# Rows loaded three blocks ahead, and the first two parts' work in another order, in a convolution and expert-MLP kernel

## The chip, the cores and the metric

The kernel runs on one core of a Trainium2 chip. The metric is the device time of one execution in microseconds (us). The engines of the core are TensorE (PE, with its weight loads shown as PEld), VectorE (DVE), ScalarE (ACT), GpSimd (POOL) and SyncE (SP). Each works through its own instructions in program order and waits on semaphores for the others. SP issues the loads (one queue, in order), POOL issues the indirect transfers that scatter rows.

## The reference

The input x has 8 sequences of 3584 tokens with 192 channels, 28672 tokens in all, in float32. First comes a causal convolution over 7 tokens whose taps are shared by the 24 channels of a head; then each token goes through one of 8 expert MLPs. A local gate decides whether the token takes its own best expert or that of the token before it, so the choice is a chain along the sequence.

```python
w = softmax(weight)                               # 8 heads x 7 taps
y[b, s, h*24:(h+1)*24] = sum_k w[h, k] * x_pad[b, s + k, h*24:(h+1)*24]

logits = y @ w_gate                               # 8 experts
local_gate = sigmoid(y @ w_local)
for b in range(B):
    prev_e = -1
    for s in range(S):
        fresh_e = argmax(logits[b, s])
        e = fresh_e if s == 0 or local_gate[b, s] < 0.5 else prev_e
        prev_e = e
        p = softmax(logits[b, s])
        out[b, s] = p[e] * (relu(y[b, s] @ w1[e]) @ w2[e])   # 192 -> 1024 -> 192
```

## The kernel before

The tokens are cut into 16 *parts* of 1792 tokens, 14 to a partition. Each part passes three steps, and the MLP follows in *blocks*.

**Convolution** (`conv`, L162). Where it is VectorE's, a head is one multiplication (`first`, on ScalarE at L177 or, for part 0, on VectorE at L175) and six multiply-adds on VectorE (L201). For parts 0 and 1, four of the eight heads (`ON_PE`: heads 5, 6, 7, 0) go to TensorE as products with diagonal matrices (L184), and ScalarE copies each result out (L187). The result is `y_sb`, whose last 64 columns repeat channels 128 to 191.

**Routing** (`route`, L262). `yr` takes channels 128 to 191 (L265), and L266 makes the repeat in `y_sb`, both on GpSimd. TensorE transposes the part (L280), ScalarE, or for every second tile of parts 0 and 1 VectorE, copies the transposes to `yT` (L282, L284), TensorE multiplies them with the gate weights (L291), ScalarE copies to `lsb` (L294, L295), TensorE transposes back (L299), VectorE takes `lt` (L303) and works through argmax, the chain along the sequence and the position of every token among those of its expert (to `posi`, L417). Then 14 *puts* are listed in `to_put`; each is one indirect transfer on GpSimd (`put`, L444) of 128 rows to their places in `slots` in DRAM, where rows lie by expert. Last come `base` (L421) and `table` (L455, some 20 small VectorE instructions), which ends in `tabi` (L512), the list of blocks that are sure to be full by then: first row and expert of each.

**Blocks.** There are 144: 35 single ones of 128 rows, 87 double ones of 256 rows, and 22 single ones at the end. Blocks 0 to 6 need part 0's rows alone, 7 to 20 part 1's too, 21 to 34 part 2's, 35 to 37 part 3's, 38 to 44 part 4's. Each block has its expert's weights `wb` (1536 KB, L565, four buffers) and rows `xg` (L572, six buffers), both loaded on SP's queue after SP has read the entry of `tabi`. `turn` transposes the rows on TensorE (L592) and VectorE copies them to `xT` (L595); `hidden` makes the hidden layer (L609, L613, Relu on ScalarE at L616); `output` multiplies back (L623), ScalarE scales with the gate (L629), and GpSimd scatters the rows to `out` (L632). Block i's instructions on TensorE are `hidden(i)`, `turn(i + 1)`, `output(i)`.

**The order.** Everything is issued in an order written out in the program, and each engine keeps to it. `conv` and `route` are generators: each yield gives the time that the instructions before it are reckoned to take on VectorE, or "hop" or "pe", where the route waits for TensorE and convolution work is put in. `step(time, scatters)` (L673) issues work of the current route and convolution up to that time, and so many puts; a single block has two steps of 2.1 with one put each, a double one two of 4.2 with one and two puts. `start_conv` (L643) also issues the load of the next part's x (L119, two buffers).

In the head (L695 to L713) part 0's route is issued with pieces of part 1's convolution at its hops; its puts follow at once, ahead of `base` and `table`; the rest of part 1's convolution comes next, then part 2's convolution is started (with it the load of x for part 3), and part 1's whole route is issued with eight pieces of part 2's convolution and its table. Its puts are left to the steps of the blocks. Then three weights and after them two blocks' rows are loaded (L728 to L731), and the blocks start.

In the loop, `ensure(i)` (L718) loads the weights of block i + 3 and then the rows of block i + 2. Where a block's part isn't routed, or some of its puts aren't issued yet, `ensure` issues steps of 4.2 until they are (L724).

Of the kernel before, what the change touches and what calls it, by code (L numbers as in the profile page):

```python
# [17 lines left out]
P = 128  # L18
B, S, D = 8, 3584, 192
# [33 lines left out]
Y0 = 2  # L53
# [29 lines left out]
def kernel(  # L83
# [8 lines left out]
    nc = tc.nc  # L92
# [31 lines left out]
    c = cst.tile([P, H, KC], F32, name="c")  # L124
# [19 lines left out]
    ON_PE = HEADS[:4]  # L144
# [117 lines left out]
    def route(g, alone):  # L262
        y_sb = got.pop(g)
        yr = yt.tile([P, NT, DR], F32, name="yr", bufs=2)
        nc.gpsimd.tensor_copy(yr, y_sb[:, :, Y0 + P:Y0 + D])  # L265
        nc.gpsimd.tensor_copy(y_sb[:, :, Y0 + D:], y_sb[:, :, Y0 + P:Y0 + D])  # L266

# [3 lines left out]
        for u in range(3):  # L271
            for jj in range(0, 4, 2):
                tps = (hps_p.tile([P, 2, BT], F32, name="hps") if alone and u else
                       bg_p.tile([P, 2, 2 * P], F32, name="bg"))
                for j in range(2):
                    for q in range(GQ):
                        t = min(2 * (4 * q + jj + j), NT - 2)
                        src = (yr[:, t:t + 2, :].rearrange("p t d -> p (t d)") if u == 2
                               else y_sb[:, t + u, Y0:Y0 + P])
                        nc.tensor.transpose(tps[:, j, q * P:(q + 1) * P], src, identity=ident)  # L280
                if alone and jj:
                    nc.vector.tensor_copy(yT[:, u, jj:jj + 2, :], tps)  # L282
                else:
                    nc.scalar.copy(yT[:, u, jj:jj + 2, :], tps)  # L284
            if not alone:
                yield "hop"
# [6 lines left out]
        m = 32 * (NP - 4)  # L293
        nc.scalar.copy(lsb[:m, :], lps[:m, :])  # L294
        nc.scalar.copy(lsb[m:, :P], lps[m:, :P])  # L295
        yield "hop"
        ltp = bg_p.tile([P, GQ * P], F32, name="bg")
        for q in range(GQ):
# [119 lines left out]
        for t in range(NT):  # L418
            to_put.append((g, y_sb[:, t, :], posi[:, t:t + 1]))
        yield 0.2  # L420
        nc.vector.tensor_tensor(base, base, nps[:, E:2 * E], op=Alu.add)  # L421
        yield 0.2
        was = g - 1 if g else None
# [8 lines left out]
    to_put = []  # L432
# [4 lines left out]
    def put():  # L437


        if not to_put:  # L440
            return
        g, rows, to = to_put.pop(0)
        nc.gpsimd.nop()
        ins = nc.gpsimd.indirect_dma_start(  # L444
            out=slots[:, :], in_=rows, in_offset=None,
            out_offset=bass.IndirectOffsetOnAxis(ap=to, axis=0)).ins
# [115 lines left out]
    def load_w(i):  # L562
        e = entry(i, 1, E - 1)
        wb = wp.tile([P, WA + WB], F32, name="wb")
        nc.sync.dma_start(out=wb, in_=w12[bass.ds(e, 1)].rearrange("o p x -> (o p) x"))  # L565
        return wb

    def load_rows(i):
        n, group = blocks[i][1], blocks[i][3]
        r = entry(i, 0, DUMMY + 1 - n)  # L570
        xg = xp.tile([P, KT, DG], F32, name="xg")
        get = nc.sync.dma_start(  # L572
            out=xg[:, :n, :].rearrange("p k d -> p (k d)"),
            in_=slots.rearrange("(r p) d -> r (p d)", p=UT)[bass.ds(r, n)]
            .rearrange("o (p x) -> (o p) x", x=n * DG))
# [22 lines left out]
    def hidden(n, wb, xT):  # L598
        hT = hp.tile([P, FK, BT], F32, name="hT")
        hps = [hps_p.tile([P, 2, BT], F32, name="hps") for q in range(FK // 2)]  # L600
        w = slice(0, n * P)


        for half in range(2):
            for j in range(2):
                for row in range(2):
                    rows = slice(row * DR, (row + 1) * DR)
                    f0 = F + (half * 2 + j) * P
                    nc.tensor.matmul(hps[half * 2 + row][:, j, w], lhsT=wb[rows, f0:f0 + P],  # L609
                                     rhs=xT[rows, 1, w], start=(j == 0), stop=False,  # L610
                                     skip_group_check=True)
# [31 lines left out]
    def start_conv(on_pe=()):  # L643
        g = st["conv"] + 1

        free = not any(p[0] <= g - 3 for p in to_put)
        if st["cgen"] is None and g < NPART and g <= st["route"] + LEAD and free:
            st["conv"] = g
            st["cgen"], st["pgen"] = conv(g, x_in.pop(g), on_pe)
            next(st["cgen"])  # L650
            if g + 1 < NPART:
                x_in[g + 1] = load_x(g + 1)

    def conv_op():
        c = next(st["cgen"], None) if st["cgen"] else None
        if c is None:
            st["cgen"] = None
        return c

    def start_route(alone=False):  # L660
        done = st["conv"] - (st["cgen"] is not None)
        if st["rgen"] is None and st["route"] < done:
            st["route"] += 1
            st["rgen"] = route(st["route"], alone)

    def route_op():
        c = next(st["rgen"], None)
        if c is None:
            st["rgen"] = None
            st["routed"] = st["route"]  # L670
        return c

    def step(time, scatters):  # L673

        start_route()
        start_conv()
        go = st["rgen"] is not None
        while time > 0:
            c = route_op() if go else conv_op()
            if c is None:  # L680
                if not go:
                    break
                go = False
            elif c == "hop":
                go = False
            elif c == "pe":
                c = conv_op()
                time -= c or 0
            else:
                time -= c  # L690
        for _ in range(scatters):
            put()


    start_route(True)  # L695
    start_conv(ON_PE)
    for g in range(2):
        while st["rgen"]:
            c_ = route_op()
            if c_ in ("hop", "pe"):  # L700
                conv_op()
            if c_ == "pe":
                for _ in range(3):
                    next(st["pgen"], None)
            while to_put and g == 0:
                put()
        for _ in st["pgen"]:
            pass
        if g == 0:
            while st["cgen"]:  # L710
# [74 lines left out]
```

## Time and profile before

| | us |
|---|---|
| time, median of 3 runs (lowest to highest) | 1500.04 (1499.82 to 1504.15) |
| the profiled execution's own time | 1495.5 |
| its span in the profile | 1493.8 |
| TensorE busy | 1443.5 (97%) |
| VectorE busy | 659.2 (44%) |
| ScalarE busy | 509.0 (34%) |
| GpSimd busy | 505.5 (34%) |

The profile records one execution. In its rows a time is counted from the span's start; a bracket at the end of a timeline row gives how long the engine sat idle before the instruction and what ended the wait. L numbers are lines of the kernel before. "issue" stands for waits that the profile doesn't explain. An average over the span hides that the stages differ: the head, where TensorE is mostly idle; the single blocks to about 330 us, with the highest traffic on the DMA queues; the double blocks, where TensorE is busy throughout; and the last single blocks.

### The profile page before, as it was taken

The page shows a single profiled execution, that of the slowest core. Times are in us where ns is not written, and L with a number is a line of the kernel's source. Part 1 is how long each engine was busy: PE and PEld are TensorE (multiplying, and loading weights), DVE is VectorE, ACT ScalarE, POOL GpSimd, SP SyncE. Part 2 cuts the span into 40 slices and gives each one's busy share as a digit, 9 for nine tenths or more (in the row PEclk, how much of TensorE's full clock was granted, in tenths as well). Part 3 has the DMA queues.
Part 4 walks back from the last instruction along what each step waited for, and adds up shares of the span by engine and source line. Part 5 has one row for each costly group of instructions (what it writes and reads, how often), then busy time and mean ns, then how long its engine had stood idle before and what let it go on. Part 6 is the DMA issues. An engine that isn't in the chain of part 4 may idle for free.

```text
span 1493.8 us, 25899 instructions
## 1 busy us (share of the span) xinstructions
PE 1443.5 (97%) x9792; PEld 1292.7 (87%) x9792; DVE 659.2 (44%) x1759; ACT 509.0 (34%) x1093; POOL 505.5 (34%) x526
## 2 busy tenths in 40 slices
PE   7588999999999999999999999999999999999998
PEld 4377898989889898898988888898898898899997
DVE  6778666666666666666666662400000000000000
ACT  3124434434343333433434333222222222223332
POOL 1433444434344343443444434343211211211111
PEclk9889999999999999999999999999999999999999
DMA  4577999987575665665656555665554554556883
GB/s 163 212 249 278 359 303 327 332 324 265 186 255 213 225 249 193 249 242 196 249 198 248 206 191 204 203 228 189 197 186 164 196 188 164 194 185 241 292 306 133
DMA packets 66415, 343.03 MB, mean 230 GB/s; under 512 B 12656, under 2 KB 23655, under 8 KB 45810
## 3 DMA queue, kind: packets, MB, share of 16 engines
q1 hardware_dynamic: 44064, 288.66, 55.5%
q0 software_dynamic: 22224, 52.70, 9.0%
q8 instruction: 78, 1.28, 0.3%
q14 instruction: 47, 0.39, 0.1%
q10 hardware_dynamic: 2, 0.00, 0.0%
HBM read 288.51 MB, written 53.49 MB: 229 GB/s over the span
## 4 chain that ended last, share of the span: by engine, by line
PE 54%; issue 30%; POOL 7%; DMA 5%; DVE 3%; POOLq 0%; SPq 0%; ACT 0%; DVEq 0%; ACTq 0%
PE yps L623 23%; PE hps L613 15%; PE hps L609 8%; POOL out_dram L632 5%; DMA xg<-slots 4%; POOL slots L444 2%; PE xps L592 2%; PE bg L280 2%; DVE y_sb L201 2%; PE bg L291 2%; PE hps L184 1%; DMA x_sb<-in_x_dram 1%; POOLq L632 0%; PE bg L299 0%; PE bg L390 0%
## 5 line engine op out<-in xcount | busy, mean ns | idle before, releaser
L623 PE MATMUL yps<-wb,hT 128*128 128x192 f32 x3696 | 626.7, 327 | 0.0
L623 PEld LDWEIGHTS yps<-wb,hT 128*128 128x128 f32 x3696 | 597.2, 190 | 1.9 <-issue 1.6
L632 POOL DMA_INDIRECT out_dram<-o_sb,xg x231 | 243.9, 1056 | 861.2 <-ACT o_sb L629 782.6
L613 PE MATMUL hps<-xT,wb 128*128 128x256 f32 (+1 forms) x2304 | 442.3, 345 | 0.0
L201 DVE SCALAR_TENSOR_TENSOR y_sb<-x_sb,c,y_sb 128x336 f32<-128x336 f32 x720 | 415.7, 587 | 25.5 <-ACT y_sb L177 8.3
L613 PEld LDWEIGHTS hps<-xT,wb 128*128 128x128 f32 x2304 | 365.0, 191 | 67.3 <-issue 29.1
L616 ACT ACTIVATE hT<-hps 128x512 f32<-128x512 f32 (+1 forms) x576 | 294.9, 512 | 348.3 <-PE hps L613 341.0
L595 DVE COPY xT<-xps 128x512 f32<-128x512 f32 (+1 forms) x144 | 84.3, 586 | 740.6 <-PE xps L592 740.6
L629 ACT ACTIVATE o_sb<-yps,xg 128x192 f32<-128x192 f32 x231 | 87.6, 418 | 554.0 <-PE yps L623 549.0
L444 POOL DMA_INDIRECT slots<-y_sb,posi x224 | 220.8, 986 | 100.8 <-issue 66.5
L609 PE MATMUL hps<-xT,wb 64*128 64x256 f32 (+1 forms) x2304 | 240.9, 349 | 6.5 <-DVE xT L595 6.5
L609 PEld LDWEIGHTS hps<-xT,wb 64*128 64x128 f32 x2304 | 183.4, 188 | 49.3 <-issue 17.3
L592 PE MATMUL xps<-ident,xg 128*128 128x128 f32 x462 | 74.8, 274 | 8.8 <-DMA xg<-slots 8.6
L592 PEld LDWEIGHTS xps<-ident,xg 128*128 128x128 f32 x462 | 57.3, 142 | 19.5 <-DMA xg<-slots 6.4
L177 ACT ACTIVATE y_sb<-x_sb,c 128x336 f32<-128x336 f32 x116 | 65.9, 580 | 0.4
L284 ACT COPY yT<-bg 128x512 f32<-128x512 f32 x86 | 46.2, 590 | 12.5 <-PE bg L280 12.5
L280 PE MATMUL bg<-ident,y_sb 128*128 128x128 f32 x240 | 33.5, 287 | 8.2 <-DVE y_sb L201 7.7
L184 PE MATMUL hps<-x_sb,wb 128*128 128x336 f32 x112 | 35.1, 473 | 3.8 <-DMA x_sb<-in_x_dram 3.8
L280 PEld LDWEIGHTS bg<-ident,y_sb 128*128 128x128 f32 x240 | 29.3, 149 | 10.2 <-issue 6.7
L184 PEld LDWEIGHTS hps<-x_sb,wb 128*128 128x128 f32 x112 | 22.3, 203 | 14.5 <-issue 5.5
L291 PE MATMUL bg<-yT,wg 128*32 128x256 f32 (+1 forms) x384 | 25.2, 371 | 0.0
L265 POOL COPY yr<-y_sb 128x896 f32<-128x896 f32 x16 | 15.2, 950 | 18.5 <-ACT y_sb L187 18.5
(137 smaller groups left out, 351.9 us busy)
## 6 DMA issues: line engine op xcount, KB each, us to landing
wb<-in_w_dram SPq DMA_DIRECT2D x144, 1536.0 KB
x_sb<-in_x_dram SPq DMA_DIRECT2D x16, 1920.0 KB
xg<-slots SPq DMA_DIRECT2D x87, 258.0 KB
xg<-slots SPq DMA_DIRECT2D x57, 129.0 KB
out_dram<-o_sb,xg POOLq DMA_INDIRECT x231
slots<-y_sb,posi POOLq DMA_INDIRECT x224
slots<-pad SPq DMA_DIRECT2D x1, 129.0 KB
slots<-pad,toi POOLq DMA_INDIRECT x8
```

Source lines behind the costliest of these rows:

```text
L184: nc.tensor.matmul(acc, lhsT=dg_of(i, k), rhs=chans(h, k), start=(k == 0), stop=(k == KC - 1))
L201: nc.vector.scalar_tensor_tensor(cols(h), chans(h, k), c[:, h, k:k + 1], cols(h), Alu.mult, Alu.add)
L280: nc.tensor.transpose(tps[:, j, q * P:(q + 1) * P], src, identity=ident)
L444: ins = nc.gpsimd.indirect_dma_start(out=slots[:, :], in_=rows, in_offset=None, out_offset=bass.IndirectOffsetOnAxis(ap=to, axis=0)).ins
L592: nc.tensor.transpose(xps[:, d, k * P:(k + 1) * P], xg[:, k, Y0 + d * P:Y0 + (d + 1) * P], identity=ident)
L595: nc.vector.tensor_copy(xT[:, :, :n * P], xps[:, :, :n * P])
L609: nc.tensor.matmul(hps[half * 2 + row][:, j, w], lhsT=wb[rows, f0:f0 + P], rhs=xT[rows, 1, w], start=(j == 0), stop=False, skip_group_chec ...
L613: nc.tensor.matmul(hps[s // 2][:, s % 2, w], lhsT=wb[:, s * P:(s + 1) * P], rhs=xT[:, 0, w], start=False, stop=True, skip_group_check=True)
L616: nc.scalar.activation(hT[:, s - 1:s + 1, w], hps[s // 2][:, :, w], Act.Relu)
L623: nc.tensor.matmul(yps[:, k, :], lhsT=hT[:, m, k * P:(k + 1) * P], rhs=wb[:, WA + m * D:WA + (m + 1) * D], start=(m == 0), stop=(m == FK - 1))
L629: nc.scalar.activation(o_sb[:, k, :], yps[:, k, :], Act.Copy, scale=gate)
L632: sent = nc.gpsimd.indirect_dma_start(out=out, in_=o_sb[:, k, :], in_offset=None, out_offset=bass.IndirectOffsetOnAxis(ap=xg.bitcast(I32)[ ...
```

## The change

Four things differ.

- **Order of the head.** Part 1's convolution is started first, and six of its VectorE steps stand ahead of part 0's route. Part 0's route is issued up to a new mark, "placed", that stands behind the listing of the puts; then its puts, the rest of part 1's convolution, and only then `base` and `table` of part 0. Part 1's route is issued to "placed" with nothing between, and four of its puts; its `base`, its `table` and the other puts are left to the steps of the blocks. Part 2's convolution, and with it the load of x for part 3, starts in the first step of block 0.
- **Part 1's copies.** In part 1's route `yr`, the repeat in `y_sb`, and all six copies to `yT` are ScalarE's; the repeat is issued behind the copies to `lsb`.
- **Rows ahead.** Rows are loaded up to three blocks ahead. The third is left for later if its part isn't routed and placed; the first two are waited for with extra steps as before.
- **Order on SP's queue.** In the loop the rows' loads are issued in front of the weights' load, which stays three blocks ahead. At the start the order is weights 0, rows 0, rows 1, weights 1, weights 2.

```diff
     def route(g, alone):
...
-        nc.gpsimd.tensor_copy(yr, y_sb[:, :, Y0 + P:Y0 + D])
-        nc.gpsimd.tensor_copy(y_sb[:, :, Y0 + D:], y_sb[:, :, Y0 + P:Y0 + D])
+
+        copy = nc.scalar.copy if alone and g else nc.gpsimd.tensor_copy
+        copy(yr, y_sb[:, :, Y0 + P:Y0 + D])
+        if not (alone and g):
+            copy(y_sb[:, :, Y0 + D:], y_sb[:, :, Y0 + P:Y0 + D])
...
-                if alone and jj:
+                if alone and g == 0 and jj:
                     nc.vector.tensor_copy(yT[:, u, jj:jj + 2, :], tps)
                 else:
                     nc.scalar.copy(yT[:, u, jj:jj + 2, :], tps)
...
         nc.scalar.copy(lsb[m:, :P], lps[m:, :P])
+        if alone and g:
+            copy(y_sb[:, :, Y0 + D:], y_sb[:, :, Y0 + P:Y0 + D])
         yield "hop"
...
             to_put.append((g, y_sb[:, t, :], posi[:, t:t + 1]))
         yield 0.2
+        yield "placed"
         nc.vector.tensor_tensor(base, base, nps[:, E:2 * E], op=Alu.add)
...
+    start_conv(ON_PE)
+    for _ in range(6):
+        conv_op()
     start_route(True)
-    start_conv(ON_PE)
-    for g in range(2):
-        while st["rgen"]:
-            c_ = route_op()
-            if c_ in ("hop", "pe"):
-                conv_op()
-            if c_ == "pe":
-                for _ in range(3):
-                    next(st["pgen"], None)
-            while to_put and g == 0:
-                put()
-        for _ in st["pgen"]:
-            pass
-        if g == 0:
-            while st["cgen"]:
-                conv_op()
-            start_route(True)
-            start_conv()
-
-    WAHEAD, AHEAD = 3, 2
+    c_ = ""
+    while c_ != "placed":
+        c_ = route_op()
+        if c_ in ("hop", "pe"):
+            conv_op()
+        if c_ == "pe":
+            for _ in range(3):
+                next(st["pgen"], None)
+    while to_put:
+        put()
+    for _ in st["pgen"]:
+        pass
+    while st["cgen"]:
+        conv_op()
+    while st["rgen"]:
+        route_op()
+    start_route(True)
+    while route_op() != "placed":
+        pass
+    for _ in range(4):
+        put()
+
+    AHEAD = 3
     wbs, xgs = {}, {}
 
     def ensure(i):
 
-        if i + WAHEAD < len(blocks):
-            wbs[i + WAHEAD] = load_w(i + WAHEAD)
-        if i + AHEAD < len(blocks):
-            g = blocks[i + AHEAD][3]
+        for j in range(len(xgs) + i, min(i + AHEAD + 1, len(blocks))):
+            g = blocks[j][3]
             while st["routed"] < g or any(p[0] <= g for p in to_put):
+                if j > i + 2:
+                    return
                 step(4.2, 1)
-            xgs[i + AHEAD] = load_rows(i + AHEAD)
-
-    for i in range(WAHEAD):
-        wbs[i] = load_w(i)
-    for i in range(AHEAD):
-        xgs[i] = load_rows(i)
+            xgs[j] = load_rows(j)
+
+    def weights(i):
+        if i < len(blocks):
+            wbs[i] = load_w(i)
+
+    weights(0)
+    for j in range(2):
+        xgs[j] = load_rows(j)
+    weights(1)
+    weights(2)
     xT = turn(blocks[0][1], xgs[0])
     for i, (_, n, _, _) in enumerate(blocks):
         ensure(i)
+        weights(i + AHEAD)
         hT = hidden(n, wbs[i], xT)
```

More of the change, by code (lines that the diff above doesn't have):

```diff
@@ L685, in step @@
                 go = False
+            elif c == "placed":
+                pass
             elif c == "pe":
@@ L692, in step @@
             put()
+    start_conv(ON_PE)
+    for _ in range(6):
+        conv_op()
     start_route(True)
-    start_conv(ON_PE)
-    for g in range(2):
-        while st["rgen"]:
-            c_ = route_op()
-            if c_ in ("hop", "pe"):
-                conv_op()
-            if c_ == "pe":
-                for _ in range(3):
-                    next(st["pgen"], None)
-            while to_put and g == 0:
-                put()
-        for _ in st["pgen"]:
-            pass
-        if g == 0:
-            while st["cgen"]:
-                conv_op()
-            start_route(True)
-            start_conv()
-    WAHEAD, AHEAD = 3, 2
+    c_ = ""
[16 more added lines that the diff above has]
+    while route_op() != "placed":
+        pass
+    for _ in range(4):
+        put()
+    AHEAD = 3
     wbs, xgs = {}, {}
     def ensure(i):
-        if i + WAHEAD < len(blocks):
-            wbs[i + WAHEAD] = load_w(i + WAHEAD)
-        if i + AHEAD < len(blocks):
-            g = blocks[i + AHEAD][3]
+        for j in range(len(xgs) + i, min(i + AHEAD + 1, len(blocks))):
+            g = blocks[j][3]
             while st["routed"] < g or any(p[0] <= g for p in to_put):
+                if j > i + 2:
+                    return
                 step(4.2, 1)
-            xgs[i + AHEAD] = load_rows(i + AHEAD)
-    for i in range(WAHEAD):
-        wbs[i] = load_w(i)
-    for i in range(AHEAD):
-        xgs[i] = load_rows(i)
+            xgs[j] = load_rows(j)
[7 more added lines that the diff above has]
+    weights(2)
     xT = turn(blocks[0][1], xgs[0])
```

## The prediction

> **What bounds the kernel now.** I read the page's head, then the busy time of each engine by stretches of the span (columns: stretch, its length, busy us of PE, PEld, DVE, ACT, POOL with instruction counts, granted clock of PE, DMA share, GB/s).
>
> ```profile
> span 1493.8 us, 25899 instructions
> ```
>
> ```profile
> 54.00:83.00 29.00, 10.24 (x59) 6.99 (x59) 18.62 (x69) 3.73 (x8) 9.62 (x10) 0.62 0.85 340
> 83.00:104.00 21.00, 20.96 (x160) 19.76 (x162) 12.66 (x24) 7.37 (x19) 6.49 (x6) 0.87 0.54 181
> 104.00:134.00 30.00, 23.79 (x194) 20.88 (x190) 25.40 (x45) 13.32 (x31) 15.47 (x15) 0.94 0.83 299
> 134.00:171.00 37.00, 36.90 (x312) 34.71 (x313) 26.37 (x87) 12.74 (x34) 11.39 (x11) 1.00 0.89 307
> 171.00:210.00 39.00, 37.35 (x332) 33.97 (x331) 26.35 (x70) 17.02 (x43) 16.57 (x17) 1.00 0.90 326
> 210.00:250.00 40.00, 37.12 (x319) 33.98 (x318) 26.71 (x58) 17.42 (x42) 19.20 (x19) 1.00 0.97 352
> 250.00:290.00 40.00, 39.57 (x338) 36.75 (x337) 27.69 (x89) 14.19 (x36) 15.77 (x15) 1.00 0.90 303
> 290.00:333.00 43.00, 41.53 (x356) 37.78 (x354) 28.38 (x74) 18.56 (x45) 16.77 (x16) 1.00 0.90 331
> 400.00:900.00 500.00, 500.00 (x3240) 447.65 (x3239) 325.50 (x867) 189.21 (x382) 217.41 (x213) 1.00 0.64 225
> ```
>
> TensorE bounds all that follows the head: 500 of 500 us busy in the stage of double blocks. What can be won is the head (block 0 starts at 83) and TensorE's idle time among the first single blocks: 6.2 + 0.1 + 1.65 + 2.9 + 0.4 + 1.5 = 12.7 us between 104 and 333. The waits of PE and its timeline name the causes:
>
> ```profile
> PE xps L592 <- DMA xg<-slots: 8.6, 8, 1.9
> ```
>
> ```profile
> 119.51 3.51 PE L280 MATMUL bg<-ident,y_sb 128*128 128x128 f32 x16 [2.53 <-DVE y_sb L201]
> ```
>
> Late rows (L592) make 8.6 us, of which 0.8 lies before block 0. The other stall stands at block 5. There rows 7, the first of part 1, are due; L724 finds part 1 neither routed nor placed and emits four extra steps of DVE work in one go. PE's transposes of part 2 then wait, and the 16 of them run slowly (below).
>
> **The head, step by step.** The timeline of part 0's route, in order of time:
>
> ```profile
> 27.35 0.58 ACT L177 ACTIVATE y_sb<-x_sb,c 128x336 f32<-128x336 f32 x1
> ...
> 30.41 0.69 DVE L282 COPY yT<-hps 128x512 f32<-128x512 f32 x1 [0.18 <-PE hps L280]
> ...
> 33.15 0.31 DVE L303 COPY lt<-bg 128x144 f32<-128x144 f32 x1 [0.97 <-PE bg L299]
> ...
> 43.39 0.17 DVE L417 CAST posi<-pos 128x14 int32<-128x14 f32 x1
> ...
> 44.60 1.19 POOL L444 DMA_INDIRECT slots<-y_sb,posi  x1 [18.95 <-DVE ends L472]
> ...
> 46.74 0.28 DVE L512 CAST tabi<-tab 128x2 int32<-128x2 f32 x1
> ...
> 47.17 9.52 DVE L201 SCALAR_TENSOR_TENSOR y_sb<-x_sb,c,y_sb 128x336 f32<-128x336 f32 x16
> ...
> 51.74 0.44 ACT L187 COPY y_sb<-hps 128x336 f32<-128x336 f32 x1 [3.51 <-PE hps L184]
> ```
>
> (1) Six L201 of part 1 now stand ahead of part 0's route: 27.93 + 6 x 0.595 (9.52/16) = 31.5; then the three DVE copies of yT, 3 x 0.69, to 33.6, where the last ended at 31.1. So part 0's chain is about 2.4 us later: posi ends at 46.0, the first put (L444) starts at 47.0, the copies of part 1's PE heads (L187) end at 54.6. **This step is a loss**, 1.7 to 2.5 us.
> (2) Eight more L201 run at hops and waits of this route as now, so 10 are left of 24 (16 now). They follow posi at once: 46.0 + 10 x 0.595 = 51.9. Part 0's table, now ahead of them, comes behind: tabi follows posi by 3.5 us now, so 55.4. Only SP's weight loads wait for it.
>
> Part 1's route, and the start of the blocks:
>
> ```profile
> 58.01 0.59 ACT L284 COPY yT<-bg 128x512 f32<-128x512 f32 x1 [4.88 <-PE bg L280]
> ...
> 61.70 0.96 POOL L444 DMA_INDIRECT slots<-y_sb,posi  x1 [0.30 <-issue]
> 62.65 0.95 POOL L265 COPY yr<-y_sb 128x896 f32<-128x896 f32 x1
> ...
> 63.65 1.12 PE L280 MATMUL hps<-ident,yr 128*128 128x128 f32 x8 [3.18 <-POOL yr L265]
> ...
> 68.84 0.31 DVE L303 COPY lt<-bg 128x144 f32<-128x144 f32 x1 [2.26 <-PE bg L299]
> ...
> 77.54 0.69 PE L592 MATMUL xps<-ident,xg 128*128 128x128 f32 x2 [0.83 <-DMA xg<-slots]
> ...
> 78.81 0.17 DVE L417 CAST posi<-pos 128x14 int32<-128x14 f32 x1
> ...
> 82.57 0.42 DVE L595 COPY xT<-xps 128x256 f32<-128x256 f32 x1
> 83.04 2.08 PE L609 MATMUL hps<-xT,wb 64*128 64x128 f32 x16 [4.81 <-DVE xT L595]
> ...
> 91.48 0.97 PEld L609 LDWEIGHTS hps<-xT,wb 64*128 64x128 f32 x16 [0.23 <-issue]
> ...
> 97.37 0.97 PEld L609 LDWEIGHTS hps<-xT,wb 64*128 64x128 f32 x16 [0.23 <-issue]
> ```
>
> Now yr stands on POOL behind 14 puts (to 62.65). Then DVE works through the whole route, conv pieces and table before it copies xT at 82.57, though rows 0 had landed by 77.5.
> (3) yr on ScalarE is not in the trace. From L187 (336 elements, 0.44) and L284 (512, 0.59) the slope is 0.85 ns, so 896 elements take 0.92; POOL's 0.95 says the same. 54.6 + 0.9 = 55.5. All six yT copies are now ACT's: 6 x 0.59 to 59.1. The second copy, into y_sb, stands behind the lsb copies on ACT; behind it waits only the Exp (L341), which isn't due yet, and the puts of part 1, queued behind part 0's.
> (4) From the last yT copy to lt it took 2.05 in part 0 (31.10 to 33.15) and 3.3 in part 1 on a slow clock (63.65 + 1.12 + a copy of 0.69 = 65.5, to 68.84). I take 2.6: lt at 61.7. From there to posi it took 10.1 with six L201 between; they are gone. That is worth nothing (they filled waits for PE) to 6 x 0.59 = 3.5; I take 2.0. So DVE is free for xT at 61.7 + 8.1 = 69.8, the remaining table work behind it.
> (5) Rows 0 wait for part 0's puts. The last ends at 61.70 + 0.96 + 2.4 = 65.1. SP's queue now, and one later wait of the same kind:
>
> ```profile
> 56.84 0.33 SPq L119 DMA_DIRECT2D x_sb<-in_x_dram  x1
> 57.91 2.05 SPq L565 DMA_DIRECT2D wb<-in_w_dram  x3
> 70.56 1.19 SPq L572 DMA_DIRECT2D xg<-slots  x2
> ```
>
> ```profile
> 126.17 0.96 POOL L444 DMA_INDIRECT slots<-y_sb,posi  x1 [0.30 <-issue]
> ```
>
> ```profile
> 132.18 0.33 SPq L572 DMA_DIRECT2D xg<-slots  x1
> ```
>
> ```profile
> 64.00:68.00 4.00, 3.48 (x31) 1.65 (x29) 1.73 (x3) 0.92 (x2) 0.47 (x1) 0.57 1.02 428
> ...
> 92.00:96.00 4.00, 4.00 (x39) 3.88 (x36) 3.01 (x7) 2.48 (x7) 3.11 (x3) 1.00 0.91 298
> ...
> 128.00:132.00 4.00, 4.00 (x41) 3.35 (x41) 3.82 (x8) 1.43 (x4) 0.00 (x0) 1.00 0.33 131
> ```
>
> Now x_sb 3 and three weights (6.7 MB) lie on the queues ahead, and the put's landing takes 7.9 us from its end (62.66 to 70.56). At 127.13 to 132.18 it took 5.05; the queues ran empty about 1.3 us into 128 to 132, 2.9 us before it ended. In the changed head only weights 0 (3.7 us at 428 GB/s, from some 56.5: 55.4 and the 1.1 that SP took from 56.84 to 57.91) are ahead, long done. So between 0 and 7.9, I take 3.0: rows 0 issued at 68.1. Their landing took 7.0 behind loads (70.56 to 77.54); on empty queues 129 KB take 0.3 us at 428 GB/s; I take 2.0. With 0.69 of transposes and 0.42 of xT, block 0 starts at 71.2, **11.8 us earlier** (7 to 14). The Trainium skill ("DMA: Bandwidth & Descriptors", Anatomy of one DMA) fits a fixed 2.0 us plus bytes at 436 GB/s per DMA, mostly the write receipt; by it the sum would be about 1 us better; no row here shows a put on idle queues.
> (6) Block 0 runs 8.44 us against block 1's 5.89 since PE has idled; it idles again, so no gain.
>
> **Among the single blocks.** Nothing of PE's work is added. Deferred are conv 2 (8 L201 done early now), table 1, ten puts and x_sb 3. Counting the yields of the steps: table 1 ends in block 0, conv 2 in block 6, puts of part 1 in block 4, of part 2 in block 18. Rows 7 and 21 are due at 5 and 19, so no extra steps are forced there (one is at block 36, in the double stage, beside 11 us of PE work). The stall at 104 to 134 goes, 6.2 us, and with it slow transposes: 16 in 3.51, where 8 take 1.12 at 63.65, so some 1.3. Rows three ahead are issued one block sooner and in front of a weight load; the other 6.5 us, stalls of at most 1.9, go. What is late next: rows 7 and 21, whose SP wait for the last put ends some 8 us into block 5 or 19 (the put ends some 3 us in, an estimate from 0.44 of ACT as L187 has it and two issues of about 1 us each with gaps; plus 5.05), land 2 us later, and are due 9 us in (5.89 and half a block): 0 to 3 us each, I take 1.5. And weights: from 68.1 the queues owe weights 1 to 3, x_sb 3, rows (7.1 MB, 16.6 us at 428) and some 1.3 MB of puts and outputs. These cost 3.0 us at 428 GB/s and 11.6 if all 8.4 MB went at the 298 of 92 to 96; I take 6.7. So weights 4 start at 91.4, about where they start now (behind block 0, 91.5), and land near 97 (3.7 us, and 1.9 for puts and outputs between); block 4 is due at 71.2 + 8.44 + 3 x 5.89 = 97.3. That is a tie until the puts end: 0 to 4 us, I take 2. Net: 12.7 + 1.3 - 3 - 2 = 9.
>
> **Sum.** 11.8 + 9 = 21 us off the profiled execution's own 1495.5 (span 1493.8 and 1.7 around it): 1474.5. The median shown, 1500.04, stands 4.5 above that execution; on its scale I forecast **1479**, 1471 to 1486 for this case alone.
>
> **The rivals.**
> A. The DMA queues pace the single blocks: what rows no longer stall, weights do. For it: share 0.89 to 0.97 there, and the tie above. Against: PE never waited for weights. It leaves the head's gain alone: 1488. The Trainium skill ("TensorE: Matmul & The Clock Gate", What's actually happening) halves the clock after an idle window of about 3.4 us; a late weight in one gap that long would cost a slow block more, 2.5 us by block 0, so 1490; single stalls up to 1.9 us left 1.00 between 171 and 250.
> B. The puts land as late as now, 7.9 us after the last: block 0 at 76, 1484.
> C. The reorder doesn't free DVE: no gain from the six L201 and the slow 3.3 us to lt: posi at 72.5, block 0 at 73.5, 1481.
> D. Slower: the queues sustain too little in the whole single stage. Now its last block ends at 331 (chain of waits):
>
> ```profile
> 328.44 2.70 PE yps L623 x16
> ```
>
> Its bytes (76.6 MB by the windows from 83) plus x_sb 3 and weights 1 and 2 must now move after 68.1: 82 MB in 263 us, so **below 312 GB/s** the changed kernel is slower; at 298, +12 us: 1512. Against: 321 GB/s are moved between 104 and 333 at a share near 0.91.
>
> **How the numbers follow.** Forecast 0.60, A 0.20, B 0.08, C 0.08, D 0.04. The range reaches over B and C and into A: 1471 to 1490. About 0.3% can be told from no change: faster 0.91, within 0.05 (a fifth of A, and the edge of D), slower 0.04 (D).
>
> **What would show it.** Right: block 0's first L609 near 71, yr on ACT near 55, rows 0 on SP's queue near 68 and weights 1 behind; no L592 waiting for xg except at blocks 7 and 21; PE's idle sum from block 0 to 333 near 5. Wrong: an L609 that waits for wb near 97 to 115 (A, D), rows 0 issued after 72 (B), xT behind posi after 72 (C).

## The result, and the profile after

| | us, median (lowest to highest) | ratio to the kernel before, 95% interval |
|---|---|---|
| kernel before, 4 runs | 1501.02 (1499.82 to 1504.15) | |
| changed kernel, 4 runs | 1467.9 (1467.07 to 1468.62) | 0.9776 [0.9759, 0.9793] |

The changed kernel is 33 us faster, not 21: the direction was right, the time lies 11.1 us below the forecast and 3 us below the range. Its profiled execution took 1467.37 us. The page's head:

```profile
span 1465.7 us, 25910 instructions
```

Where the 28.1 us between the two spans came from can be read from the starts of the blocks (their first L609, now L615). L numbers in rows of the changed kernel are its own lines: L615, L619, L598, L629 and L283 are L609, L613, L592, L623 and L280 of the kernel before. Block 0 starts 83.04 - 69.70 = **13.3 us** earlier. Block 36, the second double one, starts at 342.29 before and 313.34 now, so another **15.6 us** came between these two. Behind block 36, 0.8 us was lost.

For the stretch from block 0 to block 36, the busy times of the engines, first of the kernel before (columns as in the prediction; the first number after the length is TensorE's busy time):

```profile
83.04:342.29 259.25, 246.50 (x2049) 226.43 (x2049) 178.25 (x462) 103.01 (x250) 103.58 (x100) 0.98 0.86 306
```

and of the changed kernel:

```profile
69.70:313.34 243.64, 239.56 (x2041) 223.33 (x2041) 165.67 (x428) 104.97 (x253) 97.49 (x97) 0.99 0.91 351
```

TensorE's idle time fell from 12.75 to 4.08 us, but its busy time fell too, by 6.9 us, for nearly the same instructions. The groups of instructions by line and shape in the same two stretches show in which (busy us, mean ns of one, then the idle time before them). Before:

```profile
L623 PE MATMUL yps<-wb,hT 128*128 128x192 f32 x592 | 103.3, 328 | 0.0
L613 PE MATMUL hps<-xT,wb 128*128 128x128 f32 x560 | 73.4, 285 | 0.0
L609 PE MATMUL hps<-xT,wb 64*128 64x128 f32 x560 | 41.6, 289 | 6.5 <-DVE xT L595 6.5
L592 PE MATMUL xps<-ident,xg 128*128 128x128 f32 x76 | 14.7, 279 | 7.9 <-DMA xg<-slots 7.8
L280 PE MATMUL bg<-ident,y_sb 128*128 128x128 f32 x64 | 9.7, 306 | 2.5 <-DVE y_sb L201 2.5
```

After:

```profile
L629 PE MATMUL yps<-wb,hT 128*128 128x192 f32 x592 | 102.2, 326 | 0.0
L619 PE MATMUL hps<-xT,wb 128*128 128x128 f32 x560 | 72.6, 283 | 0.0
L615 PE MATMUL hps<-xT,wb 64*128 64x128 f32 x560 | 41.6, 289 | 1.2 <-DVE y_sb L201 0.7 <-DVE xT L601 0.5
L598 PE MATMUL xps<-ident,xg 128*128 128x128 f32 x76 | 14.2, 273 | 1.9 <-DMA xg<-slots 1.9
L283 PE MATMUL bg<-ident,y_sb 128*128 128x128 f32 x64 | 8.3, 273 | 0.7 <-DVE y_sb L201 0.7
```

(The idle time of the first instruction of a stretch counts with it: 4.8 of the 6.5 us stand ahead of block 0.) The late rows are down from 7.9 to 1.9 us, and the four groups L623, L613, L592 and L280 take 1.1, 0.8, 0.5 and 1.4 us less for the same work. In part that is the granted clock (third number from the end). Before, it stood at 0.5 over the start of block 0 and over the slow transposes of L280:

```profile
83.04:88.49 5.45, 5.45 (x32) 5.23 (x33) 0.00 (x0) 1.15 (x3) 0.00 (x0) 0.50 0.00 0
119.21:122.62 3.41, 3.11 (x14) 2.75 (x15) 3.31 (x5) 1.69 (x4) 3.10 (x4) 0.50 0.98 366
```

In the changed kernel it does so over the start of block 0 alone:

```profile
69.70:73.49 3.79, 3.79 (x24) 3.56 (x25) 0.00 (x0) 0.38 (x1) 2.88 (x4) 0.50 0.92 322
```

No wait for weights stands among TensorE's waits there.

The head of the changed kernel, from its timeline:

```profile
27.25 3.59 DVE L201 SCALAR_TENSOR_TENSOR y_sb<-x_sb,c,y_sb 128x336 f32<-128x336 f32 x6 [1.95 <-ACT y_sb L177]
...
44.85 0.17 DVE L422 CAST posi<-pos 128x14 int32<-128x14 f32 x1
...
46.07 1.19 POOL L450 DMA_INDIRECT slots<-y_sb,posi  x1 [21.13 <-ACT y_sb L187]
...
53.54 0.94 ACT L267 COPY yr<-y_sb 128x896 f32<-128x896 f32 x1
...
55.35 2.07 ACT L287 COPY yT<-hps 128x512 f32<-128x512 f32 x4
...
59.34 0.31 DVE L308 COPY lt<-bg 128x144 f32<-128x144 f32 x1 [4.80 <-PE bg L304]
...
62.86 0.96 POOL L450 DMA_INDIRECT slots<-y_sb,posi  x1 [0.30 <-issue]
...
66.42 1.19 SPq L578 DMA_DIRECT2D xg<-slots  x2
...
67.07 0.17 DVE L422 CAST posi<-pos 128x14 int32<-128x14 f32 x1
...
68.49 0.69 PE L598 MATMUL xps<-ident,xg 128*128 128x128 f32 x2 [2.65 <-DMA xg<-slots]
69.22 0.42 DVE L601 COPY xT<-xps 128x256 f32<-128x256 f32 x1 [1.98 <-PE xps L598]
69.70 2.08 PE L615 MATMUL hps<-xT,wb 64*128 64x128 f32 x16 [0.52 <-DVE xT L601]
```

Rows 0 are issued 66.42 - 63.82 = 2.6 us after the last put of part 0 ends, and are there 2.07 us later; VectorE is free for them at 67.24, 1.2 us before TensorE can begin. So the start of the blocks now hangs on part 0's puts, not on part 1's route.

### The profile page after: what moved, and what is told of

It is laid out like the page before. It is cut to its first block, busy times and chain, and to the rows that moved or that the text cites. A ratio compares the mean times of both kernels' runs of the same rounds, so it can differ in the third digit from the quotient of the medians.

```text
span 1465.7 us, 25910 instructions
## 1 busy us (share of the span) xinstructions
PE 1434.6 (98%) x9792; PEld 1288.0 (88%) x9792; DVE 650.3 (44%) x1756; ACT 512.9 (35%) x1098; POOL 499.5 (34%) x524
## 4 chain that ended last, share of the span: by engine, by line
PE 61%; issue 29%; POOL 6%; DMA 2%; DVE 1%; POOLq 0%; ACT 0%; SPq 0%; DVEq 0%; ACTq 0%
PE yps L629 25%; PE hps L619 17%; PE hps L615 9%; POOL out_dram L638 5%; PE bg L283 3%; PE xps L598 2%; PE hps L184 2%; PE bg L294 2%; POOL slots L450 2%; DVE y_sb L201 1%; DMA xg<-slots 1%; DMA x_sb<-in_x_dram 1%; POOLq L638 0%; PE bg L304 0%; PE bg L395 0%
## 5 line engine op out<-in xcount | busy, mean ns | idle before, releaser
L629 PE MATMUL yps<-wb,hT 128*128 128x192 f32 x3696 | 625.6, 326 | 0.0
L629 PEld LDWEIGHTS yps<-wb,hT 128*128 128x128 f32 x3696 | 597.2, 190 | 0.2
L638 POOL DMA_INDIRECT out_dram<-o_sb,xg x231 | 240.9, 1043 | 830.1 <-ACT o_sb L635 763.2
L619 PE MATMUL hps<-xT,wb 128*128 128x256 f32 (+1 forms) x2304 | 441.5, 345 | 0.0
L619 PEld LDWEIGHTS hps<-xT,wb 128*128 128x128 f32 x2304 | 364.2, 191 | 67.3 <-issue 29.0
L201 DVE SCALAR_TENSOR_TENSOR y_sb<-x_sb,c,y_sb 128x336 f32<-128x336 f32 x720 | 411.1, 581 | 19.5 <-ACT y_sb L177 2.4
L622 ACT ACTIVATE hT<-hps 128x512 f32<-128x512 f32 (+1 forms) x576 | 295.5, 513 | 344.5 <-PE hps L619 337.4
L615 PE MATMUL hps<-xT,wb 64*128 64x256 f32 (+1 forms) x2304 | 240.9, 349 | 1.2 <-DVE y_sb L201 0.7
L615 PEld LDWEIGHTS hps<-xT,wb 64*128 64x128 f32 x2304 | 183.4, 188 | 43.4 <-issue 17.2
L598 PE MATMUL xps<-ident,xg 128*128 128x128 f32 x462 | 74.3, 273 | 4.6 <-DMA xg<-slots 4.6
L598 PEld LDWEIGHTS xps<-ident,xg 128*128 128x128 f32 x462 | 57.9, 142 | 13.7 <-DMA xg<-slots 2.7
L177 ACT ACTIVATE y_sb<-x_sb,c 128x336 f32<-128x336 f32 x116 | 65.9, 579 | 0.4
L283 PE MATMUL bg<-ident,y_sb 128*128 128x128 f32 x240 | 31.2, 273 | 1.8 <-DVE y_sb L201 0.7
L283 PEld LDWEIGHTS bg<-ident,y_sb 128*128 128x128 f32 x240 | 27.5, 141 | 3.4 <-issue 1.1
L294 PEld LDWEIGHTS bg<-yT,wg 128*32 128x32 f32 x384 | 12.3, 109 | 9.7 <-issue 3.3
```

The costliest lines, as they stand in the source:

```text
L201: nc.vector.scalar_tensor_tensor(cols(h), chans(h, k), c[:, h, k:k + 1], cols(h), Alu.mult, Alu.add)
L598: nc.tensor.transpose(xps[:, d, k * P:(k + 1) * P], xg[:, k, Y0 + d * P:Y0 + (d + 1) * P], identity=ident)
L629: nc.tensor.matmul(yps[:, k, :], lhsT=hT[:, m, k * P:(k + 1) * P], rhs=wb[:, WA + m * D:WA + (m + 1) * D], start=(m == 0), stop=(m == FK - 1))
L638: sent = nc.gpsimd.indirect_dma_start(out=out, in_=o_sb[:, k, :], in_offset=None, out_offset=bass.IndirectOffsetOnAxis(ap=xg.bitcast(I32)[ ...
```

## The experiments

The experiments ran on four chips, called P, Q, R and S here. Kernels of one group share the runs of the kernel before; "the change" is the changed kernel, unaltered. From chip to chip only the ratios are compared.

| chip | kernel | median us | ratio, 95% interval |
|---|---|---|---|
| P (before 1503.92) | before, once more | 1504.52 | 1.0008 [0.9999, 1.0018] |
| P | head_only | 1496.6 | 0.9956 [0.9943, 0.997] |
| P | loop_only | 1491.4 | 0.9921 [0.9907, 0.9934] |
| P | a_weights_first | 1485.98 | 0.9886 [0.9871, 0.9901] |
| Q (before 1497.65) | the change | 1467.95 | 0.9802 [0.9788, 0.9815] |
| Q | a_weights_first2 | 1471.85 | 0.983 [0.9816, 0.9843] |
| Q | a_no_six | 1470.16 | 0.9816 [0.9803, 0.983] |
| Q | before_4puts | 1502.29 | 1.0024 [1.0008, 1.004] |
| R (before 1503.18) | the change | 1481.1 | 0.9854 [0.9836, 0.9871] |
| R | head_only2 | 1493.23 | 0.9939 [0.9923, 0.9956] |
| R | loop_only2 | 1489.51 | 0.9912 [0.9896, 0.9928] |
| R | a_old_copies | 1484.46 | 0.9881 [0.9862, 0.9899] |
| S (before 1502.79) | the change | 1481.57 | 0.9855 [0.9832, 0.9878] |
| S | a_ahead2 | 1481.7 | 0.9855 [0.9832, 0.9878] |
| S | loop_4puts | 1481.13 | 0.9849 [0.9825, 0.9873] |
| S | a_two_puts | 1500.15 | 0.9981 [0.9966, 0.9997] |
| S again (before 1505.2) | the change | 1483.85 | 0.9855 [0.9835, 0.9875] |
| S again | loop_4puts2 | 1483.61 | 0.9851 [0.9832, 0.9869] |

### The two halves alone

head_only has the head of the change and the loads of before; loop_only the head of before and the loads of the change (with weights 0 to 2 ahead of rows 0 and 1 at the start).

```diff
# head_only, against the change
-    AHEAD = 3
+    WAHEAD, AHEAD = 3, 2
...
+        if i + WAHEAD < len(blocks):
+            wbs[i + WAHEAD] = load_w(i + WAHEAD)
+        if i + AHEAD < len(blocks):
+            g = blocks[i + AHEAD][3]
...
# loop_only, against before
+        for j in range(len(xgs) + i, min(i + AHEAD + 1, len(blocks))):
...
+        weights(i + AHEAD)
```

> The new order of the head with part 1's copies on ScalarE and its four early puts; loads as in the kernel before (three weights, then two rows; in the loop weights before rows, rows two ahead). My account: head about 8 us earlier (the 13.3 of the full change less some 5 because rows 0 wait behind three weights), the forced steps at block 5 gone (some 7), the late rows kept: 1501 - 15 = 1486. Rival, rows ahead are worth nothing: 1468 to 1473. Rival, all the gain in the single blocks comes from the loads: 1493.

> The kernel before with the new loop alone: rows up to three ahead and in front of the weights. My account: the waits for xg go (8.6 us of idle time in the profile, 7.8 behind block 0), the forced steps at block 5 stay: 1501 - 8 = 1493. Rival, TensorE's idle time understates these stalls and rows ahead bring most of the 14.8 us won behind block 0: 1486 to 1489. Rival, they bring nothing because weights become late: 1501.

Measured: the head alone 7.3 us, the loop alone 12.5 us less than before on P; 10.0 and 13.7 us on R, where the whole change wins 22.1. Both expectations missed: 15 us for the head, 8 for the loop. On R the halves add up to 23.6, and the loop is the larger one, although its late rows looked like only 7.8 us. The stretch from block 0 to block 36 in loop_only:

```profile
82.96:335.36 252.40, 246.54 (x2048) 225.17 (x2048) 177.05 (x462) 102.06 (x250) 101.64 (x100) 0.98 0.89 315
```

The kernel before on the same chip took 265.82 us for it, with 249.33 busy. Of the 13.4 us, 10.6 are idle time and 2.8 busy time. Ahead of L592 TensorE sat idle for 9.0 us in the kernel before on P, 8.1 of them for late rows, and not at all in loop_only, so rows three ahead and in front of the weights do what was said of them. In the head alone, the reverse: it starts block 7 at 125.50 against 141.32, 15.8 us ahead, but is only 11.0 us ahead at block 36 (337.73 against 348.68) and 10.8 at its end. Of the 4.9 us lost between, 3.5 are idle time and 1.4 busy time. The idle time ahead of the rows' transposes stays (7.5 us, 7.9 in the kernel before). That ahead of `output`, for `hT`, the hidden layer that ScalarE writes (L616, now L622), rises from 0.7 to 3.4; more of it below.

### The order of the first loads

```diff
# a_weights_first and a_weights_first2, against the change
-    weights(0)
+    for i in range(3):
+        weights(i)
     for j in range(2):
         xgs[j] = load_rows(j)
-    weights(1)
-    weights(2)
```

> The changed kernel with the first loads in the old order: weights 0, 1, 2, then rows 0 and 1. My account: the last put of part 0 lands under load as before (5 to 8 us after its end instead of 2.6), rows 0 land behind three weights, block 0 starts 4 to 6 us later, and nothing of it is won back: 1472 to 1474. Rival, the weights have to be moved anyway and the single blocks are paced by the queues: 1468.

> The same kernel as a_weights_first, beside the changed kernel on one chip. Theory 1: 1486, with block 0 at 78. Theory 2: 1468 to 1474 or as far above the changed kernel as the late rows cost, 4 to 6 us.

On Q it costs 3.9 us. The timeline of a_weights_first2 (loads, then TensorE's transposes of rows 0):

```profile
72.88 3.14 SPq L578 DMA_DIRECT2D xg<-slots  x4
...
75.32 0.69 PE L598 MATMUL xps<-ident,xg 128*128 128x128 f32 x2 [9.09 <-DMA xg<-slots]
```

With two more weight loads (3.1 MB) on the queues, part 0's puts land later: rows 0 are issued at 72.88, 9.0 us after the last put's end, instead of at 66.51, 1.8 us after it, in the change on this chip. TensorE waits 9.09 us for them, and block 0 starts at 76.53 where the change on this chip has 69.79. This is rival B as a kernel. Of the 6.7 us, 3.3 are left at block 36 (317.32 against 314.07) and at the end; the expectation that nothing is won back was wrong. On P the change itself did not run; a_weights_first's ratio lies 0.003, some 5 us, above those of the change on R and S.

### The six early steps of part 1

```diff
# a_no_six, against the change
-    for _ in range(6):
-        conv_op()
```

> The changed kernel without the six steps of part 1's convolution ahead of part 0's route. By the prediction's step 1 they are a loss of 1.7 to 2.5 us: puts and rows 0 come 2 us earlier, and block 0 starts 1 to 2 us earlier (part 1's route is then what ends last): 1466 to 1467. Rival, VectorE stands idle at hops instead and part 1's convolution ends later: no gain or a loss of 1 us.

Without them the kernel is 2.2 us slower on Q, and block 0 starts at 73.34, 3.6 us later. Its timeline shows why:

```profile
52.74 0.57 ACT L177 ACTIVATE y_sb<-x_sb,c 128x336 f32<-128x336 f32 x1
53.35 3.59 DVE L201 SCALAR_TENSOR_TENSOR y_sb<-x_sb,c,y_sb 128x336 f32<-128x336 f32 x6 [3.34 <-ACT y_sb L177]
...
57.09 1.94 PE L283 MATMUL bg<-ident,y_sb 128*128 128x128 f32 x8 [4.72 <-DVE base L427]
```

Part 0's puts do start earlier (45.27 against 46.94). But the last head's `first` (L177) now stands on ScalarE behind the copies of TensorE's heads; VectorE waits 3.34 us for it, and part 1's transposes begin at 57.09 and the first eight take 1.94 us, where the change on this chip has 54.57 and 1.09. The prediction's step (1) called the six steps a loss; they are a gain.

### Part 1's copies as before

```diff
# a_old_copies, against the change
-        copy = nc.scalar.copy if alone and g else nc.gpsimd.tensor_copy
+        copy = nc.gpsimd.tensor_copy
...
-                if alone and g == 0 and jj:
+                if alone and jj:
```

> The changed kernel with part 1's copies as in the kernel before: yr and the repeat on GpSimd, every second yT copy on VectorE. yr then stands behind 14 puts (to about 64 instead of 54 us), lt comes some 8 us later, posi near 75, and block 0 starts near 76 instead of 69.8: 1473 to 1475. Rival, rows 0 and the blocks' own waits hide it: 1468 to 1470.

On R this costs 3.4 us: `yr` on GpSimd starts at 64.46, behind the puts, and block 0 at 80.18 instead of 76.23. Most of the 4 us stay to the end (spans 1482.7 and 1479.1).

### Four puts early, with and without rows ahead

before_4puts is the kernel before with four of part 1's puts ahead of the first loads. loop_4puts is loop_only with the same line.

```diff
+    for _ in range(4):
+        put()
+
```

> The kernel before with four puts of part 1 issued in the head, so that no steps are forced at block 5; nothing else differs. My account: the stall at blocks 4 and 5 goes, 7 us (two idle stretches of 2.5 and 1.6 us, the slow transposes, 0.6): 1496. Rival, the four steps' work has to be done anyway and the wait only moves: 1502.

> The kernel before with the new loop and four puts of part 1 in the head: no steps forced at block 5, rows ahead. Alone, the four puts brought nothing (1.0024) and the loop 12 to 14 us. Theory 1, the forced steps cost 7 us once late rows no longer take it back: 0.986 to 0.988 of the kernel before, with block 7 some 7 us earlier than in the loop alone. Theory 2, they cost nothing: 0.991 to 0.992.

Four early puts spare the four steps that L724 forces at block 5. In before_4puts they do: block 7 starts at 132.10, against 140.21 in the first profile of before. But nothing is won in the end, 1502.29 against 1497.65. TensorE's waits say where it went (us in total, times, longest):

```profile
PE xps L592 <- DMA xg<-slots: 20.0, 17, 3.1
```

Late rows cost 20.0 us there, against 8.6 in the first profile of the kernel before; this was the slowest of its six executions (1495.84 to 1505.47). With rows ahead the picture turns. In loop_only2 the forced steps stand in TensorE's timeline as

```profile
117.56 1.09 PE L280 MATMUL bg<-ident,y_sb 128*128 128x128 f32 x8 [2.72 <-DVE y_sb L201]
...
131.96 1.16 PE L609 MATMUL hps<-xT,wb 64*128 64x128 f32 x16 [1.70 <-DVE xT L595]
```

4.4 us of waits, yet blocks 4 and 5 take 23.1 us there (108.87 to 131.96) and 12.7 in loop_4puts (110.58 to 123.24); block 6 is 1.5 us longer there. As ratios, though of different chips, loop_4puts stands at 0.985 and loop_only at 0.991 to 0.992: about 10 us. From block 0 to the end the two profiles of loop_only took 1406.7 and 1404.4 us, those of loop_4puts 1395.5 and 1398.5. So the forced steps cost some 6 to 11 us, but one gets them only once rows no longer come late: alone, the early puts gave nothing.

### Two blocks ahead, or three

```diff
# a_ahead2, against the change
-        for j in range(len(xgs) + i, min(i + AHEAD + 1, len(blocks))):
+        for j in range(len(xgs) + i, min(i + 3, len(blocks))):
```

> The changed kernel with rows two blocks ahead, still in front of the weights. Theory 1, the place in SP's queue does it: rows no longer wait behind a weight load that itself waits for a buffer, so they are issued a block sooner even at two ahead, and the third block adds nothing: within 1 us of the changed kernel. Theory 2, the third block is needed: waits for xg come back, 3 to 6 us slower.

1481.7 against 1481.57: on S the third block is worth nothing. Of the loads' part that leaves the place in front of the weights on SP's queue, where each weight load waits until a buffer is free: head_only2, with rows as far ahead but behind the weights, is 12 us slower than the change on R, and the order of the first loads makes up only 4 to 5 of that.

### More puts per step

```diff
# a_two_puts, against the change
-        step(2.1 * n, 1)
+        step(2.1 * n, 2)
```

> The changed kernel with two puts instead of one in the first step of each block, so that a part's rows are complete about two blocks sooner. Rows 7 (and 21, 38) are then not the last to come: 1 to 3 us faster than the changed kernel. Rival, the puts crowd the queues while they are full: same or slower.

A miss: 18.6 us slower than the change. The profiled execution was its fastest (spans 1493.1 and 1480.0). Of the 13.1 us there, 3.1 are lost by block 3, no more by block 36, and 10 between blocks 36 and 100. TensorE's timeline shows waits in both stages:

```profile
95.33 0.92 PE L629 MATMUL yps<-wb,hT 128*128 128x192 f32 x4 [1.52 <-issue]
```

```profile
934.35 1.09 PE L283 MATMUL bg<-ident,y_sb 128*128 128x128 f32 x8 [1.69 <-DVE y_sb L201]
```

By the program, puts that go sooner start the next convolution sooner (`start_conv` waits for them), and the whole written order shifts. In the double stage each part's transposes now stand right behind their last L201, and TensorE waits about 0.5 us for it once in every 62 us, at the end 1.69. Those nine waits sum to 5.6 us between blocks 36 and 100; three more, ahead of L629 and not explained by the profile, sum to 2.9, and TensorE's busy time is 2.6 longer (775.46 against 772.85), with 1.0 less of waits for `hT`. There is a rival: VectorE's waits for which the profile names no releaser (next section) are far more here than in the change beside it, which has 4 of 14.0 us in all:

```profile
DVE xT L601 <- remote: 84.9, 14, 7.6
```

Whether two puts lose as much on a chip without such waits wasn't tried.

### Why the same kernel takes 1468 us on one chip and 1481 on another

> The changed kernel unchanged, as the measure for the run beside it. It gave 1467.9 and 1468.0 us on two occasions and 1481.1 and 1481.6 on two others. Where ScalarE's copies of yT in part 1's route stand back to back (55 to 57.5 us) I expect 1468 and block 0 near 70; where they stand apart (57.6 to 62.7) 1481 and block 0 near 76.

> The kernel before with rows three ahead in front of the weights and four puts of part 1 ahead of the loads, so without the new order of the head and without the copies on ScalarE. On the last occasion it equalled the changed kernel (1481.1 against 1481.6), though its block 0 began 8 us later. Theory 1: the head's new order is worth its 8 to 13 us, but only where ScalarE's copies run undisturbed; if the changed kernel beside it takes 1468, this one takes 1476 to 1481. Theory 2: what the head wins is lost again among the single blocks whatever happens, because the queues and the order of the steps set the pace there; then this kernel equals the changed one within 2 us here too.

loop_4puts has neither the new order of the head nor the copies on ScalarE. On S its block 0 starts 6.9 us after that of the change (82.82 and 75.96), and yet both take the same time, twice. From block 0 to the last block, TensorE of the change on S (the first two numbers: the length of the stretch, then TensorE's busy time):

```profile
sum 1393.64, PE 1383.55 PEld 1250.79 DVE 596.99 ACT 483.84 POOL 476.10; mean PE 345.89 PEld 312.70 DVE 149.25 ACT 120.96 POOL 119.03
```

and of loop_4puts2:

```profile
sum 1386.97, PE 1385.30 PEld 1251.35 DVE 605.04 ACT 485.26 POOL 474.36; mean PE 346.33 PEld 312.84 DVE 151.26 ACT 121.31 POOL 118.59
```

10.1 us idle against 1.7, and those 8.4 us are more than the 6.9: the lead of the head is lost among the blocks. The groups of the change on S, block 0 to 34, name the wait:

```profile
L629 PE MATMUL yps<-wb,hT 128*128 128x192 f32 x539 | 94.8, 328 | 6.7 <-ACT hT L622 6.7
```

On Q the same kernel in the same blocks:

```profile
L629 PE MATMUL yps<-wb,hT 128*128 128x192 f32 x539 | 93.2, 326 | 0.0
```

It is ScalarE that is late with `hT`. The timeline on S in block 13:

```profile
163.79 0.38 PE L598 MATMUL xps<-ident,xg 128*128 128x128 f32 x2
164.97 0.39 ACT L622 ACTIVATE hT<-hps 128x256 f32<-128x256 f32 x1 [3.63 <-PE xps L598]
165.41 0.92 PE L629 MATMUL yps<-wb,hT 128*128 128x192 f32 x4 [1.23 <-ACT hT L622]
166.32 0.94 ACT L622 ACTIVATE hT<-hps 128x256 f32<-128x256 f32 x3 [0.97 <-remote]
166.48 0.42 DVE L601 COPY xT<-xps 128x256 f32<-128x256 f32 x1 [3.78 <-remote]
```

and on Q at the same place:

```profile
159.33 1.66 ACT L622 ACTIVATE hT<-hps 128x256 f32<-128x256 f32 x4 [1.37 <-PE hps L619]
160.41 0.38 PE L598 MATMUL xps<-ident,xg 128*128 128x128 f32 x2
```

On S ScalarE and VectorE sit idle for 3.6 and 3.8 us ahead of their work on these blocks, on Q for 1.4 and 1.5: some 2.3 us longer. Part of that is after what they wait for is done: VectorE starts `xT` 2.3 us after TensorE's transposes end (164.17), on Q at once (160.82, after 160.79). "remote" means that the profile names no releaser on this core. The waits of this kind for `hT` come again 61.2 and 122.4 us later (226.56 and 287.83), so they hang on a place in the program's cycle. Waits with no releaser come in the head too, on R and S, in ScalarE's copies of part 1. In the first profile of the change on S:

```profile
58.06 0.59 ACT L287 COPY yT<-hps 128x512 f32<-128x512 f32 x1 [1.92 <-PE hps L283]
59.50 0.59 ACT L287 COPY yT<-hps 128x512 f32<-128x512 f32 x1 [0.86 <-remote]
60.92 0.59 ACT L287 COPY yT<-hps 128x512 f32<-128x512 f32 x1 [0.84 <-remote]
63.05 0.59 ACT L287 COPY yT<-hps 128x512 f32<-128x512 f32 x1 [1.54 <-PE bg L294]
66.79 0.37 ACT L297 COPY lsb<-bg 96x256 f32<-96x256 f32 x1 [3.16 <-remote]
```

where the first profile has all four in 2.07 us. That is why block 0 starts at 76 there and at 70 on Q and in the first comparison. VectorE's waits of this kind over the whole profile (us in total, times, longest), of the change on S, of loop_4puts2 beside it and of the kernel before on P:

```profile
DVE xT L601 <- remote: 37.2, 9, 5.0
DVE xT L595 <- remote: 64.6, 19, 5.3
DVE xT L595 <- remote: 38.2, 12, 4.9
```

All profiles taken on P, R and S have such waits, whatever the kernel; none of those taken on Q or in the first comparison has one. What they cost TensorE doesn't follow their sum: loop_4puts2 has more of them than the change and loses less. Each chip but S was used on one occasion only, so chip and occasion can't be told apart. So of the two theories, on S the lead of the head is lost among the blocks, but the wait that takes it is for ScalarE, not for the queues that theory 2 named. Whether it stays where the engines don't stand still wasn't tried: loop_4puts never ran on such a chip. No kernel was faster than the change clear of noise.

## Why the prediction was right in its direction and wrong in its size

Of the 11.1 us, 1.5 are the head, 5.8 the single blocks, and about 4 the level.

- **Head: 13.3 us, forecast 11.8.** What set the start is the puts of part 0. The last ended at 63.82 and not 65.1, because posi came at 44.85 and not 46.0; it landed 2.6 us later and not 3.0; the rows took 2.07 us (2.0). Part 1's route gained more, but has 1.2 us to spare: yr took 0.94 us (0.92), the last four copies of yT 2.07, 0.52 each and not the 0.59 of a single one, and lt came at 59.34 (61.7), 1.9 us behind the last of them and not 2.6. The Trainium skill ("DMA: Bandwidth & Descriptors", Anatomy of one DMA) fits a fixed 2.0 us plus bytes at 436 GB/s to transfers that GpSimd issues: an estimate of 2.3 us for a put of 129 KB. By it the sum would have been 0.7 us better, not about 1. The trace has 2.6 from the end of the last put to the rows' issue, and 1.8 on Q.
- **Step (1), wrong.** It counted what six L201 cost VectorE ahead of part 0's route, and not what they spare behind it: without them the last `first` on ScalarE is late (a_no_six, 2.2 us slower).
- **Steps (3) to (5), right.** Without them block 0 starts 4.0 us later (a_old_copies) and 6.7 us later (a_weights_first2), and 3.4 and 3.9 us of that are left in the time. Rival C (posi at 72.5) did not come: 67.07. Rival B did not: 2.6 us, not 7.9.
- **Step (6)** put block 0 at no gain. It took 7.65 us instead of 8.44, with the granted clock at 0.5 for its first 3.8 us instead of 5.4. On Q it took 8.42, so the 0.8 us don't come each time.
- **Single blocks: 14.8 us, forecast 9; this is the step that failed.** In its sum, "12.7 + 1.3 - 3 - 2", the waits come out nearly right: TensorE's idle time fell by 8.7 us, where 12.7 - 3 - 2 makes 7.7. The new stalls came to 4.1 us, 1.3 of them at rows 7, none at rows 21 and none for weights; the 2 us argued from a tie didn't come, and the queues moved 351 GB/s from block 0 to block 36, where the kernel before moved 306. The term that was mis-sized is the busy time: 1.3 us of slow transposes was all that was to go, and 6.9 went. 1.4 are those transposes, as forecast. 0.8 is the hidden layer of block 0 at half the clock (L613 took 3.68 us there, now 2.89). 1.1 comes from 12 blocks of the kernel before in which a small routing matmul stands right ahead of `output`: its first matmul takes 409 or 430 ns there and 328 in all others and in the changed kernel. 0.5 is L592. 1.4 is routing work now done behind block 36, where the 0.8 us was lost. The remaining 1.7 lies in no group: neighbouring groups overlap by that much more.
- **The level.** 4.5 us were added because the profiled execution of the kernel before lay below its median. That of the changed kernel lies 0.5 us below its own. On P the profiled execution of the unchanged kernel before had a span of 1502.8 instead of 1493.8: 6.6 us more from block 0 to block 36 (3.7 idle, 2.8 busy) and 2.6 behind. But P is another chip, and one with the waits that have no releaser, so how executions on one chip differ isn't shown; what is shown is that the offset was no scale that carries over. Without it the forecast would have been 1474.5, 6.6 us off.
- **Rivals A and D** needed weights that come late or less than 312 GB/s; neither is seen.
- **Not foreseen:** that the size depends on the chip or the occasion. On R and S the forecast of 1479 would have been within 0.4% (1481.1 to 1483.85), but by luck, for another reason than the one given: there ScalarE is late in the head and among the blocks.

## What to carry to other kernels

The idle time of the bounding engine (8.7 us less here) doesn't tell all that removing its waits gives: sum its busy time for the same instructions before and after, too, and read the granted clock over the stretch. Two causes of lateness hide each other: early puts alone gave nothing, with the rows ahead some 6 to 11 us, so a repair that shows nothing alone may still be half of one that does. A load that depends on little belongs ahead of a load that waits for a buffer on the same queue; its place mattered, and one block more of distance did not, where it was tried.

## What was not expected of the hardware

The same changed kernel took 1467.9 us in the first comparison and 1467.95 on Q, and 1481.1 to 1483.85 on R and S, at a granted clock of 0.995 to 0.996 and of 0.991 to 0.993; the kernel before took 1497.65 to 1505.2 on all of them. On the slower ones ScalarE and VectorE are late together at the same places of the program, by some 2.3 us in block 13, with no releaser in the profile. The queues were no busier there: around block 13 their share was 0.77 on S and 0.88 on Q. Nor do the queues that the profile calls instruction differ: around block 13 both chips have one transfer on each of the two. The cause stays open.
